# RWKV-7 and a routed expert layer on one core: the triangular inverse by 32x32 blocks in place of 128x128 block diagonal operands

## The chip, the core and the metric

The kernel runs on one core of a Trainium2 chip. The metric is the device time of one execution in microseconds; lower is better. All data are fp32 where the rows say f32. In the rows PE is TensorE's matmul, PEld its weight load, DVE VectorE, ACT ScalarE, POOL GpSimd, SP SyncE.

## What is computed

Two layers follow each other. The first is the RWKV-7 recurrence over 768 steps, for 4 batch elements and 8 heads of 40 features; its output, 3072 rows of 320 features, goes through a router that sends each row to one of 8 experts.

```python
for t in range(S):                      # 768 steps, per batch element and head
    y[t]  = r[t] @ state.T
    Sa    = state @ a[t]
    state = state * w[t] - outer(Sa, b[t]) + outer(v[t], k[t])
x = y as (3072, 320)
logits = normalised(x) @ normalised(expert_emb).T / tau
e = argmax(logits); gate = softmax(logits)[e]
out = gate * (relu(x @ w1[e]) @ w2[e])
```

## The kernel before, in words

The recurrence is taken in chunks of L = 32 steps. With the decays of a chunk multiplied into a, k and b, a chunk needs the inverse of a unit lower triangular 32x32 matrix I + tril(a b'), per head, and after it only small matrix products with the state. A tile holds four chunks of one batch element side by side on the 128 partitions; there are 24 tiles. The matrix between the steps of a tile is therefore block diagonal: four blocks of 32x32 in 128x128, for each of 8 heads.

`prepare` (line 192) does all of a tile that needs no state: the decays (lines 199 to 231), the turned inputs `ln`, `an`, `kn`, `bn` (237), the masked products `ne`, `ge`, `fe` (248, 251), then the inverse (286 to 306), then `te`, `gv` and `pt` (306 to 324). `advance` (326) carries the state through the tile's four chunks: per chunk `u_ps` (349), `un` (353), `s_ps` (357 and 362), the new state (367, 368), the turned state `sn` (374, 376) and `y_ps` (378); after the chunks come `ut`, `he` and the last part of `y_ps` (387 to 391), the router's logits and the store of `x_rows` (397 on). While a tile is in `advance`, the next is in `prepare`: both are generators, called in turn, and a scheduler lays the instructions of both out on each engine's queue, which the engine then runs in that order.

The inverse is grown by doubling the block size, in four levels after a first step (loop at line 294). The current inverse, transposed, stands compactly in `xt`, 128 partitions by 8 heads by 32 columns. One level is:

- VectorE turns `xt` in 32x32 blocks into `xn` (281), and GpSimd spreads `xn` into the block diagonal `xe`, 128x128 per head, with zeros off the diagonal (270, called at 295).
- TensorE takes 8 products, one per head, of the block diagonal `ne` with `xt` into `w_ps` (298); ScalarE copies them to `ws` (300).
- TensorE takes 8 products of `xe` with `ws` into `x_ps` (303); VectorE puts the level's entries into `xt` (304).

So a tile has 8 such groups of products, four of `w_ps` and four of `x_ps`. In the trace each fp32 product is two matmuls with a weight load each: 8 products are 16 matmuls. These are called passes here. Rows give the block of the array that a pass uses as rows times columns: 128\*128 for `w_ps`, 40\*32 for `u_ps`.

The expert stage (line 573 on) comes after all tiles: 31 blocks of 128 rows, each gathered, multiplied by its expert's two matrices, and scattered.

Of the kernel before, what the change touches and what calls it, by code (L numbers as in the profile page):

```python
# [14 lines left out]
AX = mybir.AxisListType  # L15
PSUM = bass.MemoryType.PSUM
CMAGIC = 12582912.0
# keeps a square root's argument in range; its root is lost in the 1e-6 that is added
TINY = 1e-30
P = 128  # L20
L = 32
NCK = P // L


def bc(ap, shape, axis):
    return ap.unsqueeze(axis).to_broadcast(shape)
# [3 lines left out]
def kernel(  # L30
# [12 lines left out]
    moe_w2: bass.AP,  # L43
    out: bass.AP,
):
    """RWKV-7 state recurrence in chunks of L steps, then top-1 routed experts.

    With lam_t the product of a chunk's decays before step t, per channel e,
        at = a lam_t,  kt = k / lam_(t+1),  bt = b / lam_(t+1)
        U  = (I + tril(at bt'))^-1 (at S' + tril(at kt') V)  # L50
        y  = lam (r S + tril(r V') kt - tril(r U') bt)
        S <- (S + V' kt - U' bt) lam_L
    where S is the state at the chunk's start and tril is strict.  A tile holds four chunks of
    one batch element on 128 partitions, so that matrices between steps are block diagonal.
    The kernel carries -U.  The inverse grows from blocks of one step to blocks of L steps:
    the off-diagonal block of a pair of inverted blocks X is that of X N X.
    """
    nc = tc.nc
    B, NT, D, H, _ = rT.shape
    S = NT * P  # L60
    N = B * S
# [33 lines left out]
    with ExitStack() as attn:  # L95
        cst = attn.enter_context(tc.tile_pool(name="cst", bufs=1))
        one = attn.enter_context(tc.tile_pool(name="one", bufs=1))
        two = attn.enter_context(tc.tile_pool(name="two", bufs=2))
# [3 lines left out]
        def bank(name):  # L102
            return mmp.tile([P, 512], FP32, tag="mm", name=name)

# [1 line left out]
        blk = cst.tile([P, P], FP32, name="blk")  # L106
        nc.vector.memset(blk, 0.0)
        for c in range(NCK):
# [28 lines left out]
        for j in range(L.bit_length() - 1):  # L137
            m = cst.tile([P, L], I32, name=f"level{j}")
# [7 lines left out]
        first = cst.tile([D, W1C], FP32, name="first")  # L146
# [2 lines left out]
        decay = cst.tile([D, W1C], FP32, name="decay")  # L149
        nc.vector.memset(decay[:, 0 :: L + 1], 0.0)  # L150

# [1 line left out]
        emb = two.tile([P, XW], FP32, tag="xr", name="emb")[0:E, 0:DM]  # L153
        nc.sync.dma_start(out=emb, in_=moe_expert_emb)
        tau = cst.tile([E, 1], FP32, name="tau")
# [15 lines left out]
        def h3(t):  # L171
            return t[:, 0:DM].rearrange("p (h d) -> p h d", h=H)

        def half(t):
            return t.rearrange("p (h x) -> p h x", h=4)

        state = {}
# [12 lines left out]
            loaded[g] = d  # L190

        def prepare(g, d):
            """Everything of a tile that needs no state, in parts."""
            d.update(loaded.pop(g))
            ck = "p (x t) -> p x t"

            # products of decays: before a step, and after it to the chunk's end
            body = decay[:, 0 : W1C - 1].rearrange(ck, t=L + 1)
            nc.scalar.copy(body[:, :, 1:], d["w"].rearrange("p h (c t) -> p (h c) t", t=L))
            lam = one.tile([D, W1C], FP32, tag="lam", name="lam")  # L200
            suf = one.tile([D, W1C], FP32, tag="suf", name="suf")
            nc.vector.tensor_tensor_scan(
                lam, decay, first, initial=0.0, op0=ALU.mult, op1=ALU.add
# [26 lines left out]
            nc.gpsimd.tensor_tensor(d["k"], d["k"], d["w"], ALU.mult)  # L230
            nc.gpsimd.tensor_tensor(d["b"], d["b"], d["w"], ALU.mult)

            # steps on partitions
            for nm, src in (("ln", lx), ("an", d["a"]), ("kn", d["k"]), ("bn", d["b"])):
                ps = h3(bank(f"{nm}_ps"))
                for h in range(H):
# [5 lines left out]
            def between(nm, lhs, rhs, mask, pool):  # L242
                t = pool.tile([P, H, P], FP32, tag=nm, name=nm)
                for q in range(2):
                    ps = half(bank(f"{nm}_ps"))
                    for j in range(4):
                        h = 4 * q + j
                        nc.tensor.matmul(  # L248
                            ps[:, j], lhsT=lhs[:, h], rhs=rhs[:, h], start=True, stop=True
                        )  # L250
                    nc.vector.tensor_tensor(
                        t[:, 4 * q : 4 * q + 4], ps, bc(mask, [P, 4, P], 1), ALU.mult
                    )
                return t

            d["between"] = between
            ne = between("ne", d["a"], d["b"], nlower, one)
# [7 lines left out]
            def c3(t):  # L265
                return t[:, 0 : H * L].rearrange("p (h j) -> p h j", h=H)

            def block_diagonal(x, nm):
                t = one.tile([P, H, P], FP32, tag=nm, name=nm)
                nc.gpsimd.tensor_tensor(  # L270
                    t.rearrange("p h (c j) -> p h c j", c=NCK),
                    bc(x, [P, H, NCK, L], 2),
                    bc(blk.rearrange("p (c j) -> p c j", c=NCK), [P, H, NCK, L], 1),
                    ALU.mult,
                )
                return t

            # inverse of I - N, transposed
            def turned(x):
                t = two.tile([P, H, L], FP32, tag="xn", name="xn")  # L280
                nc.vector.transpose(  # L281
                    t.rearrange("p h j -> p (h j)"), x.rearrange("p h j -> p (h j)")
                )
                return t

            xt = two.tile([P, H, L], FP32, tag="xt", name="xt")
# [5 lines left out]
            nc.vector.copy_predicated(xt, bc(levels[0], [P, H, L], 1), turned(nn))  # L292
            yield
            for m in levels[1:]:
                xe = block_diagonal(turned(xt), "xe")
                ps = c3(bank("w_ps"))
                for h in range(H):
                    nc.tensor.matmul(ps[:, h], lhsT=ne[:, h], rhs=xt[:, h], start=True, stop=True)  # L298
                ws = two.tile([P, H, L], FP32, tag="ws", name="ws")
                nc.scalar.copy(ws, ps)  # L300
                ps = c3(bank("x_ps"))
                for h in range(H):
                    nc.tensor.matmul(ps[:, h], lhsT=xe[:, h], rhs=ws[:, h], start=True, stop=True)  # L303
                nc.vector.copy_predicated(xt, bc(m, [P, H, L], 1), ps)  # L304
                yield
            te = block_diagonal(xt, "te")
# [10 lines left out]
            for q in range(2):  # L317
                ps = half(bank("pt_ps"))
                for j in range(4):
                    h = 4 * q + j  # L320
# [3 lines left out]
                nc.scalar.copy(pt[:, 4 * q : 4 * q + 4], ps[0:D])  # L324

        def advance(g, d):
            """Four chunks through the state; the tile's rows of x, their gates and experts."""
            b, i = groups[g]
            u_ps = h3(acc.tile([P, 512], FP32, tag="u", name="u_ps"))
            y_ps = h3(acc.tile([P, 512], FP32, tag="y", name="y_ps"))  # L330
            for h in range(H):
                nc.tensor.matmul(
                    u_ps[:, h], lhsT=d["te"][:, h], rhs=d["gv"][:, h],
                    start=(h == 0), stop=False, skip_group_check=True,
                )
            for h in range(H):
                nc.tensor.matmul(
                    y_ps[:, h], lhsT=d["fe"][:, h], rhs=d["kn"][:, h],
                    start=(h == 0), stop=False, skip_group_check=True,
# [3 lines left out]
            for c in range(NCK):  # L343
                r0 = L * c
                rows = slice(r0, r0 + L)
                last = i == NT - 1 and c == NCK - 1
                st = state[b]
                for h in range(H):
                    nc.tensor.matmul(  # L349
                        u_ps[rows, h], lhsT=d["pt"][:, h, rows], rhs=st[:, h],  # L350
                        start=False, stop=True, skip_group_check=True,
                    )
                nc.vector.tensor_scalar(un[rows], u_ps[rows], -1.0, None, ALU.mult)
                if not last:
                    s_ps = h3(acc.tile([P, 512], FP32, tag="s", name="s_ps"))[0:D]
                    for h in range(H):
                        nc.tensor.matmul(  # L357
                            s_ps[:, h], lhsT=d["kn"][rows, h], rhs=d["vn"][rows, h],
                            start=(h == 0), stop=False, skip_group_check=True,
                        )  # L360
                    for h in range(H):
                        nc.tensor.matmul(  # L362
                            s_ps[:, h], lhsT=d["bn"][rows, h], rhs=un[rows, h],
                            start=False, stop=True, skip_group_check=True,
# [12 lines left out]
                for h in range(H):  # L377
                    nc.tensor.matmul(  # L378
                        y_ps[rows, h], lhsT=d["r"][:, h, rows], rhs=sn[:, h],
                        start=False, stop=False, skip_group_check=True,  # L380
# [3 lines left out]
            for q in range(2):  # L384
                ps = half(bank("ut_ps"))
# [4 lines left out]
            for h in range(H):  # L390
                nc.tensor.matmul(
                    y_ps[:, h], lhsT=he[:, h], rhs=d["bn"][:, h],
                    start=False, stop=True, skip_group_check=True,
                )
            xr = two.tile([P, XW], FP32, tag="xr", name="xr")
            x = xr[:, 0:DM]
            nc.vector.tensor_tensor(h3(xr), y_ps, d["ln"], ALU.mult)

            # logits times the row's norm, the first of the largest, the gate
            xt_ps = bank("xt_ps")  # L400
            for j, (k0, kn) in enumerate(KC):
                nc.tensor.transpose(xt_ps[0:kn, j * P : j * P + P], xr[:, k0 : k0 + kn], ident)
# [4 lines left out]
            for j, (_, kn) in enumerate(KC):  # L407
                nc.tensor.matmul(
                    lg_ps, lhsT=xs[0:kn, j], rhs=embT[0:kn, j],
                    start=(j == 0), stop=(j == len(KC) - 1),  # L410
# [34 lines left out]
        for _ in prepare(0, ready):  # L445
            pass
        for g in range(NG):
            now, ready = ready, {}
            ahead = prepare(g + 1, ready) if g + 1 < NG else iter(())
            for _ in advance(g, now):  # L450
                next(ahead, None)
                next(ahead, None)
            for _ in ahead:
                pass
            if g % 2 == 1 and g // 2 < E:
                load_w2(g // 2)
# [7 lines left out]
        )  # L464
        nc.scalar.dma_start(out=w1_sb[0 : KC[2][1], e, 2], in_=moe_w1[e, 2 * P : DM])

# [1 line left out]
    with ExitStack() as rt:  # L468
        rp = rt.enter_context(tc.tile_pool(name="rp", bufs=1))
        rps = rt.enter_context(tc.tile_pool(name="rps", bufs=1, space=PSUM))  # L470
# [15 lines left out]
        for e in range(1, E):  # L486
# [3 lines left out]
        before = rp.tile([P, P], FP32, name="before")  # L490
# [7 lines left out]
            rk, lhsT=ones, rhs=cumx.rearrange("p s e -> p (s e)"),  # L498
            start=True, stop=False, skip_group_check=True,
# [3 lines left out]
            start=False, stop=True, skip_group_check=True,  # L503
# [16 lines left out]
        off = rp.tile([P, E], FP32, name="off")  # L520
# [11 lines left out]
        nc.vector.scalar_tensor_tensor(  # L532
            out=lo, in0=bk, scalar=-float(P), in1=dest, op0=ALU.mult, op1=ALU.add
        )
        # tokens as two parts under 64, which bfloat16 holds exactly, as it does 0 and 1
        shp = [P, NSLOT, NBLK]
        bm = rp.tile(shp, FP32, name="bm")
        nc.vector.tensor_tensor(bm, bc(io_p[:, 0:NBLK], shp, 1), bc(bk, shp, 2), ALU.is_equal)
# [11 lines left out]
        for s in range(NSLOT):  # L550
            nc.tensor.matmul(
                inv, lhsT=oh[:, s], rhs=rr[:, s].rearrange("p t k -> p (t k)"),
                start=(s == 0), stop=(s == NSLOT - 1),
# [16 lines left out]
        nc.vector.tensor_reduce(n1.unsqueeze(2), cm, axis=AX.X, op=ALU.add)  # L570
        nc.vector.tensor_scalar(eblk, n1, -1.0, None, ALU.add)

# [1 line left out]
    fw = ctx.enter_context(tc.tile_pool(name="fw", bufs=2))  # L574
    xins = [fw.tile([P, XW], FP32, name=f"xin{j}", bufs=1) for j in range(XBUF)]
    for t in xins:
# [140 lines left out]
```

## Time and profile before

| what | value |
|---|---|
| runs | 2609.22 and 8315.88 us, median 5462.55 |
| span of the profiled execution | 2610.3 us |
| TensorE busy in the span | 2519.8 us, 97% |
| mean granted TensorE clock | 0.589 of full speed |
| recurrence, up to the last store of `x_rows` | 0 to about 2212 us |
| expert stage | about 2213 to 2610 us |

The span, from the first instruction to the last, lies 1 us from the shorter of the two runs, so nothing of weight lies around it. The median of two runs is their mean and says nothing of either. A granted clock of 1.00 is 2.4 GHz, one of 0.50 is 1.2 GHz. The time that a row gives for matmuls goes to the modelled end of the last; where passes follow each other without a break, the distance from one start to the next is (time of n passes less the mean of one) / (n - 1).

### The profile page before, as it was taken

What the parts mean: (1) busy time and instruction counts of PE and PEld (TensorE: products, weight loads), DVE (VectorE), ACT (ScalarE), POOL (GpSimd) and SP (SyncE); (2) the same over time, 40 slices, a digit from 0 to 9 for tenths busy, and PEclk for the clock granted to TensorE, in tenths of its full rate; (3) what the DMA queues carried; (4) which work ended last, traced back from release to release, by engine and by line L of the source; (5) the groups of instructions that cost most, each with busy time, mean ns of one, the idle gap of its engine ahead of it and who ended that gap; (6) DMA issues with size and microseconds to landing.
All of it is one profiled execution on the core that took longest, in us unless ns stands there. A gap on an engine that the chain in (4) does not pass through costs nothing. (4 is left out here: it accounts for less than half of the span.)

```text
span 2610.3 us, 35907 instructions
## 1 busy us (share of the span) xinstructions
PE 2519.8 (97%) x15728; PEld 2211.9 (85%) x15728; DVE 692.9 (27%) x1374; ACT 375.9 (14%) x769; POOL 542.8 (21%) x336
## 2 busy tenths in 40 slices
PE   6999999999999999999999999999999998699998
PEld 5999999999999999999999999999999997255554
DVE  4232232233223223312322331332233122211111
ACT  1011111011111101111110111111011102011111
POOL 3122212212211221221122122212211210211111
PEclk9655555555555555555555555555555555799999
DMA  6000000000000000000000000000000001400000
GB/s 199 11 21 9 16 19 13 14 16 21 9 16 19 12 15 16 21 9 16 19 13 14 16 21 9 16 19 13 13 19 19 6 4 33 155 26 28 23 21 6
DMA packets 28411, 62.65 MB, mean 24 GB/s; under 512 B 4052, under 2 KB 18398, under 8 KB 28256
## 3 DMA queue, kind: packets, MB, share of 16 engines
q1 hardware_dynamic: 16320, 39.88, 5.0%
q10 hardware_dynamic: 8960, 12.58, 1.6%
q0 software_dynamic: 2976, 7.89, 1.0%
q8 instruction: 126, 2.06, 0.3%
q14 instruction: 29, 0.24, 0.0%
HBM read 53.60 MB, written 9.02 MB: 24 GB/s over the span
## 5 line engine op out<-in xcount | busy, mean ns | idle before, releaser
L270 POOL TENSOR_TENSOR xe<-xn,blk 128x1024 f32<-128x1024 f32 x96 | 226.9, 2364 | 1194.9 <-DVE xn L281 1011.3
L298 PE MATMUL w_ps<-xt,ne 128*128 128x32 f32 x1536 | 352.4, 403 | 3.2 <-DVE xt L304 3.2
L303 PE MATMUL x_ps<-ws,xe 128*128 128x32 f32 x1536 | 346.9, 402 | 8.1 <-ACT ws L300 7.3
L303 PEld LDWEIGHTS x_ps<-ws,xe 128*128 128x128 f32 x1536 | 334.7, 330 | 16.8 <-issue 7.4
L298 PEld LDWEIGHTS w_ps<-xt,ne 128*128 128x128 f32 x1536 | 336.4, 329 | 13.8 <-DVE xt L304 4.0
L618 PE MATMUL h_ps<-w_sb,xT 128*128 x372 | 184.6, 622 | 8.0 <-DMA w_sb<-in_moe_w_dram 8.0
L618 PEld LDWEIGHTS h_ps<-w_sb,xT 128*128 128x128 f32 x372 | 63.1, 189 | 113.7 <-issue 109.1
L304 DVE COPY_PREDICATED xt<-level,x_ps 128x256 f32<-128x256 int32 x96 | 42.4, 442 | 418.3 <-PE x_ps L303 418.3
L357 PE MATMUL s_ps<-vn,kn 32*40 32x40 f32 x1472 | 142.6, 265 | 0.0
L367 DVE TENSOR_TENSOR st<-s_ps,st 40x320 f32<-40x320 f32 x92 | 44.4, 483 | 367.0 <-PE s_ps L362 367.0
L300 ACT COPY ws<-w_ps 128x256 f32<-128x256 f32 x96 | 35.7, 372 | 728.4 <-PE w_ps L298 728.4
L645 PE MATMUL y_ps<-w_sb,hT 128*128 x496 | 138.8, 433 | 0.0
L376 ACT COPY sn<-sn_ps 40x320 f32<-40x320 f32 x96 | 40.2, 419 | 613.7 <-PE sn_ps L374 613.7
L357 PEld LDWEIGHTS s_ps<-vn,kn 32*40 32x40 f32 x1472 | 112.3, 171 | 19.0 <-issue 5.4
L349 PE MATMUL u_ps<-st,pt 40*32 40x40 f32 x1536 | 125.9, 264 | 0.0
L378 PE MATMUL y_ps<-sn,in_r 40*32 40x40 f32 x1536 | 122.6, 265 | 0.0
L378 PEld LDWEIGHTS y_ps<-sn,in_r 40*32 40x32 f32 x1536 | 106.6, 163 | 17.7 <-issue 13.2
L645 PEld LDWEIGHTS y_ps<-w_sb,hT 128*128 128x128 f32 x496 | 91.7, 190 | 34.2
L349 PEld LDWEIGHTS u_ps<-st,pt 40*32 40x32 f32 x1536 | 106.9, 162 | 16.2 <-issue 9.4
L362 PE MATMUL s_ps<-un,bn 32*40 32x40 f32 x1472 | 116.9, 263 | 0.4 <-DVE gs L434 0.4
L362 PEld LDWEIGHTS s_ps<-un,bn 32*40 32x40 f32 x1472 | 105.9, 176 | 7.1 <-issue 4.5
L248 PE MATMUL fe_ps<-in_r,in_v 40*128 40x128 f32 x384 | 105.7, 444 | 0.0
(180 smaller groups left out, 3301.4 us busy)
## 6 DMA issues: line engine op xcount, KB each, us to landing
w_sb<-in_moe_w_dram ACTq DMA_DIRECT2D x8, 1280.0 KB
w_sb<-in_moe_w_dram SPq DMA_DIRECT2D x8, 1024.0 KB
x_rows<-xr SPq DMA_DIRECT2D x24, 160.5 KB
in_w<-in_wT_dram SPq DMA_DIRECT2D x24, 160.0 KB
in_a<-in_aT_dram SPq DMA_DIRECT2D x24, 160.0 KB
in_k<-in_kT_dram SPq DMA_DIRECT2D x24, 160.0 KB
in_b<-in_bT_dram SPq DMA_DIRECT2D x24, 160.0 KB
in_v<-in_vT_dram SPq DMA_DIRECT2D x24, 160.0 KB
```

What stands on the lines that cost most here:

```text
L248: nc.tensor.matmul(ps[:, j], lhsT=lhs[:, h], rhs=rhs[:, h], start=True, stop=True)
L270: nc.gpsimd.tensor_tensor(t.rearrange("p h (c j) -> p h c j", c=NCK), bc(x, [P, H, NCK, L], 2), bc(blk.rearrange("p (c j) -> p c j", c=NCK ...
L298: nc.tensor.matmul(ps[:, h], lhsT=ne[:, h], rhs=xt[:, h], start=True, stop=True)
L303: nc.tensor.matmul(ps[:, h], lhsT=xe[:, h], rhs=ws[:, h], start=True, stop=True)
L304: nc.vector.copy_predicated(xt, bc(m, [P, H, L], 1), ps)
L349: nc.tensor.matmul(u_ps[rows, h], lhsT=d["pt"][:, h, rows], rhs=st[:, h], start=False, stop=True, skip_group_check=True,)
L357: nc.tensor.matmul(s_ps[:, h], lhsT=d["kn"][rows, h], rhs=d["vn"][rows, h], start=(h == 0), stop=False, skip_group_check=True,)
L362: nc.tensor.matmul(s_ps[:, h], lhsT=d["bn"][rows, h], rhs=un[rows, h], start=False, stop=True, skip_group_check=True,)
L367: nc.vector.tensor_tensor(new, s_ps, st, ALU.add)
L378: nc.tensor.matmul(y_ps[rows, h], lhsT=d["r"][:, h, rows], rhs=sn[:, h], start=False, stop=False, skip_group_check=True,)
L618: nc.tensor.matmul(ps, lhsT=d["xT"][0:kn, c], rhs=w1f[0:kn, ds(ek * (len(KC) * F) + c * F + q * 512, 512)], start=(c == 0), stop=(c == len ...
L645: nc.tensor.matmul(ps, lhsT=d["hT"][:, c], rhs=w2f[:, ds(d["ek"] * (FC * DM) + c * DM, DM)], start=(c == 0), stop=(c == FC - 1),)
```

## The change

`ne` is no longer used whole. Each head's product becomes four, one per diagonal block: weights, moving operand and result are those of one block, 32x32, on its 32 partitions. The second operand of the second product is `xd`, the turned `xt` itself, so the block diagonal `xe` is not built in the loop any more; `te` is still built that way once a tile. Lines after the loop move by 10.

```diff
             for m in levels[1:]:
-                xe = block_diagonal(turned(xt), "xe")
+                xd = turned(xt)
                 ps = c3(bank("w_ps"))
                 for h in range(H):
-                    nc.tensor.matmul(ps[:, h], lhsT=ne[:, h], rhs=xt[:, h], start=True, stop=True)
+                    for c in range(NCK):
+                        rows = slice(L * c, L * c + L)
+                        nc.tensor.matmul(
+                            ps[rows, h], lhsT=ne[rows, h, rows], rhs=xt[rows, h],
+                            start=True, stop=True, skip_group_check=True,
+                        )
                 ws = two.tile([P, H, L], FP32, tag="ws", name="ws")
                 nc.scalar.copy(ws, ps)
                 ps = c3(bank("x_ps"))
                 for h in range(H):
-                    nc.tensor.matmul(ps[:, h], lhsT=xe[:, h], rhs=ws[:, h], start=True, stop=True)
+                    for c in range(NCK):
+                        rows = slice(L * c, L * c + L)
+                        nc.tensor.matmul(
+                            ps[rows, h], lhsT=xd[rows, h], rhs=ws[rows, h],
+                            start=True, stop=True, skip_group_check=True,
+                        )
                 nc.vector.copy_predicated(xt, bc(m, [P, H, L], 1), ps)
                 yield
```

The scheduler lays the queues out anew. On TensorE's queue, in a tile in the middle of the program, the first two levels stood like this before; `x8` counts products, and `st_...` is the state of one batch element after one chunk:

```order
L374 MATMUL sn_ps<-ident,st_10036 40x40 x8
L298 MATMUL w_ps<-xt,ne 128x32 x8
L362 MATMUL s_ps<-un,bn 40x40 x8
L378 MATMUL y_ps<-sn,in_r 32x40 x8
L303 MATMUL x_ps<-ws,xe 128x32 x8
L357 MATMUL s_ps<-vn,kn 40x40
L349 MATMUL u_ps<-st_10118,pt 32x40 x8
L357 MATMUL s_ps<-vn,kn 40x40 x5
L298 MATMUL w_ps<-xt,ne 128x32 x8
L357 MATMUL s_ps<-vn,kn 40x40 x2
L362 MATMUL s_ps<-un,bn 40x40 x8
L303 MATMUL x_ps<-ws,xe 128x32 x8
```

The same two levels of a tile on TensorE's queue of the changed kernel:

```order
L384 MATMUL sn_ps<-ident,st_13532 40x40 x8
L300 MATMUL w_ps<-xt,ne 32x32
L388 MATMUL y_ps<-sn,in_r 32x40 x8
L300 MATMUL w_ps<-xt,ne 32x32 x8
L372 MATMUL s_ps<-un,bn 40x40 x8
L300 MATMUL w_ps<-xt,ne 32x32 x23
L310 MATMUL x_ps<-ws,xn 32x32 x32
L359 MATMUL u_ps<-st_13614,pt 32x40 x8
L367 MATMUL s_ps<-vn,kn 40x40 x6
L300 MATMUL w_ps<-xt,ne 32x32 x32
L367 MATMUL s_ps<-vn,kn 40x40 x2
L372 MATMUL s_ps<-un,bn 40x40 x4
```

The 8 products of a group are 32 now. In the first level the products of the state that stood between `w_ps` and `x_ps` have moved into `w_ps`, and `x_ps` follows `w_ps` at once.

The last level on TensorE's queue, before:

```order
L303 MATMUL x_ps<-ws,xe 128x32 x8
L357 MATMUL s_ps<-vn,kn 40x40 x6
L298 MATMUL w_ps<-xt,ne 128x32 x8
L357 MATMUL s_ps<-vn,kn 40x40 x2
L303 MATMUL x_ps<-ws,xe 128x32 x8
```

And the last level in the changed kernel:

```order
L310 MATMUL x_ps<-ws,xn 32x32 x32
L367 MATMUL s_ps<-vn,kn 40x40 x4
L372 MATMUL s_ps<-un,bn 40x40 x4
L300 MATMUL w_ps<-xt,ne 32x32 x32
L372 MATMUL s_ps<-un,bn 40x40 x4
L310 MATMUL x_ps<-ws,xn 32x32 x32
```

Four products stand between `w_ps` and `x_ps` where two stood. On GpSimd's queue a tile was

```order
L270 TENSOR_TENSOR xe<-xn,blk 128x1024 x4
L215 TENSOR_TENSOR in_w<-suf,inv_l 40x1024
L230 TENSOR_TENSOR in_k<-in_k,in_w 40x1024
L270 TENSOR_TENSOR te<-xt,blk 128x1024
L231 TENSOR_TENSOR in_b<-in_b,in_w 40x1024
L287 COPY xt<-icomp 128x256
```

and is, in the changed kernel, without the four `xe` and with `te` ahead of `in_w`:

```order
L270 TENSOR_TENSOR te<-xt,blk 128x1024
L215 TENSOR_TENSOR in_w<-suf,inv_l 40x1024
L287 COPY xt<-icomp 128x256
L230 TENSOR_TENSOR in_k<-in_k,in_w 40x1024
L231 TENSOR_TENSOR in_b<-in_b,in_w 40x1024
```

The four `xe` are gone, and `te` no longer stands behind `in_w` and `in_k`.

## Rows read from the trace of the kernel before

**Rows 1.** The page: busy time by engine, then granted clock in 40 slices.

```profile
PE 2519.8 (97%) x15728; PEld 2211.9 (85%) x15728; DVE 692.9 (27%) x1374; ACT 375.9 (14%) x769; POOL 542.8 (21%) x336
...
PEclk9655555555555555555555555555555555799999
```

**Rows 2.** Stretches: us; busy PE, PEld, DVE, ACT, POOL; granted clock; DMA; GB/s.

```profile
1085.40:1177.30 91.90, 91.12 (x610) 85.17 (x609) 25.43 (x48) 13.34 (x28) 19.66 (x10) 0.50 0.06 15
1177.30:1268.90 91.60, 90.82 (x611) 85.03 (x610) 25.43 (x48) 13.34 (x28) 19.66 (x10) 0.50 0.05 15
2250.00:2537.00 287.00, 287.00 (x975) 152.25 (x974) 49.30 (x125) 43.74 (x76) 48.50 (x48) 1.00 0.07 23
```

**Rows 3.** Waits: who waited for whom, us, times, longest.

```profile
POOL xe L270 <- DVE xn L281: 1011.3, 75, 25.4
ACT ws L300 <- PE w_ps L298: 728.4, 96, 15.8
...
PE x_ps L303 <- ACT ws L300: 7.3, 25, 0.6
```

**Rows 4.** Groups by line: busy us, mean ns of one, idle before.

```profile
L298 PE MATMUL w_ps<-xt,ne 128*128 128x32 f32 x1536 | 352.4, 403 | 3.2 <-DVE xt L304 3.2
L303 PE MATMUL x_ps<-ws,xe 128*128 128x32 f32 x1536 | 346.9, 402 | 8.1 <-ACT ws L300 7.3 <-POOL xe L270 0.8
...
L270 POOL TENSOR_TENSOR xe<-xn,blk 128x1024 f32<-128x1024 f32 x96 | 226.9, 2364 | 1194.9 <-DVE xn L281 1011.3 <-DVE lam_l L210 183.6
...
L349 PE MATMUL u_ps<-st,pt 40*32 40x40 f32 x1536 | 125.9, 264 | 0.0
```

**Rows 5.** TensorE in order of time, a tile's first level: start, us, passes.

```profile
1105.82 1.27 PE L349 MATMUL u_ps<-st,pt 40*32 40x40 f32 x16
1107.02 0.35 PE L357 MATMUL s_ps<-vn,kn 32*40 32x40 f32 x2
1107.30 0.72 PE L374 MATMUL sn_ps<-ident,st 40*40 40x40 f32 x8
1107.95 3.62 PE L298 MATMUL w_ps<-xt,ne 128*128 128x32 f32 x16
1111.50 1.29 PE L362 MATMUL s_ps<-un,bn 32*40 32x40 f32 x16
```

**Rows 6.** The same view, later in that tile: 8 columns against 128-wide weights.

```profile
1172.17 1.00 PE L408 MATMUL lg_ps<-embT,xs 128*128 128x8 f32 x4
```

**Rows 7.** Groups by line in 1172.1 to 1174.3: mean ns of one.

```profile
L408 PE MATMUL lg_ps<-embT,xs 128*128 128x8 f32 x4 | 1.0, 361 | 0.0
```

**Rows 8.** TensorE in order of time, first tile, alone: group after group.

```profile
41.58 3.60 PE L298 MATMUL w_ps<-xt,ne 128*128 128x32 f32 x16
45.73 3.59 PE L303 MATMUL x_ps<-ws,xe 128*128 128x32 f32 x16 [0.55 <-ACT ws L300]
```

**Rows 9.** A stretch of 2 us at the higher clock.

```profile
173.50:175.50 2.00, 2.00 (x36) 1.95 (x35) 1.50 (x1) 1.99 (x7) 0.00 (x0) 1.00 0.00 0
```

**Rows 10.** TensorE in that stretch, in order of time.

```profile
175.32 0.47 PE L349 MATMUL u_ps<-st,pt 40*32 40x40 f32 x8
```

**Rows 11.** Groups by line in 175.3 to 175.75: mean ns of one.

```profile
L349 PE MATMUL u_ps<-st,pt 40*32 40x40 f32 x8 | 0.5, 201 | 0.0
```

**Rows 12.** TensorE in order of time: where the second and the last tile's `prepare` begin.

```profile
83.00 0.69 PE L237 MATMUL ln_ps<-ident,lx 40*128 40x40 f32 x8
...
2088.45 0.69 PE L237 MATMUL ln_ps<-ident,lx 40*128 40x40 f32 x8
```

## The prediction, made before the changed kernel ran

> **What bounds the kernel now.** I read the page first: TensorE is busy for 97% of the span, no other engine for more than 27%, and from the third slice to the end of the recurrence the granted clock stands near half [rows 1]. Then the stretches: two tiles in the middle have TensorE busy 91.12 of 91.90 us at a granted clock of 0.50, 1.2 GHz, while the experts run at 1.00, 2.4 GHz [rows 2]. So the recurrence is a queue of TensorE work without gaps, (2088.45 - 83.00) / 22 = 91.2 us a tile [rows 12]. The waits agree: the longest are those of GpSimd and ScalarE for work ahead of them, and TensorE waited for ScalarE's `ws` 7.3 us in all [rows 3]. The change touches one stage only, the inverse; the experts' 400 us stay.
>
> What does a pass cost there? For `w_ps`, 16 passes take 3.62 us with 0.402 for one, so the next starts (3.62 - 0.40) / 15 = 0.214 us after the last [rows 4, 5]. These passes move 32 columns. `lg_ps` moves 8 against weights as wide, and its passes follow at (1.00 - 0.361) / 3 = 0.213 [rows 6, 7]. So the moving columns are not what costs: the load of 128 weight columns is, 1.67 ns a column. `u_ps`, with 32 weight columns and 40 moving ones, goes at (1.27 - 0.264) / 15 = 0.067, which is 1.67 ns for each of 40 [rows 4, 5]. A pass thus takes 1.67 ns for each column of the larger of the two, and the other is hidden. A group of `w_ps` or `x_ps` is 16 x 0.214 = 3.42 us, and 8 of them are 27.4 of a tile's 91.2 us.
>
> **The change, part by part.**
>
> The products. A group has 32 products, 64 passes, of 32 weight columns and 32 moving ones. One after the other these take 32 x 1.67 = 0.0533 us each, and 64 of them 3.41 us: exactly what the group costs now. A quarter of the width and four times the number cancel. All that can be won is that passes on different blocks, which share neither rows nor columns of the array, run side by side. No row of before has two such passes in succession, so I bound it. Above: 0.0533 us a pass, no overlap, nothing won. Below: four abreast, 0.0533 / 4 = 0.0133, a group of 0.85 us. Four abreast is unlikely from the order itself: the two passes of a product stand next to each other on the same block and cannot overlap, so that only the second pass of one block and the first of the next can, which halves the cost at best, to 0.027, as long as starts are in order. The quickest succession of fp32 passes with their loads in any row is that of `u_ps` in a short stretch at the higher clock: (0.47 - 0.201) / 7 = 0.038 us [rows 9 to 11]. Loads and matmuls can be fed at least that fast. I take 0.038: between the ends, and what a row has shown. A group is then 64 x 0.038 = 2.43 us, 0.99 less, and 8 groups give 7.9 us a tile.
>
> The page "TensorE: Matmul & The Clock Gate" of the Trainium skill (Part 3: Packing small matmuls) says that matmuls on different 32x32 blocks start some 4 ns apart, and gives 10.6 times the rate for 16 blocks with 512 moving columns. It says nothing of two-pass fp32 products with 32 columns, and no run here shows it. The same section says that a weight load overlaps with a matmul under way only where their rows differ. The trace speaks against that: `w_ps` loads and multiplies on the same 128 rows, and in turn they would take 0.213 + 0.053 = 0.267 us, where 0.214 is measured [rows 5].
>
> Changes of block shape. Between passes of different shape the array stands still for a moment: 16 passes of `u_ps` from 1105.82 would end their turn at 1106.89, and `s_ps` starts at 1107.02; `w_ps` from 1107.95 at 1111.37, and `s_ps` starts at 1111.50 [rows 5]. That is 0.13 us each. In the new order a tile has 43 of them where it had 42, so 0.1 us a tile is added.
>
> Waits. In the first level the changed order puts `x_ps` straight behind `w_ps`. The first tile shows what that costs: `x_ps` starts 45.73 - 41.58 = 4.15 us after `w_ps`, and 4.15 - 15 x 0.214 = 0.94 us after its last pass [rows 8]. Of these 0.05 are the last pass itself, so 0.9 us are lost per tile, with all of the state's products queued behind on TensorE and nothing else waiting that is late. In the last level four products, 8 passes, stand between: 8 x 0.067 + 2 x 0.13 = 0.80 of the 0.94, so 0.15 is lost. At the other levels the products between cover it. Together with the shapes that is 1.2 us a tile.
>
> GpSimd. 96 `xe` of 2.36 us go, 227 us of GpSimd's time [rows 4]. TensorE waited for them 0.8 us in the whole run, so their cover is TensorE's own queue and I count nothing. `te` moves ahead, which nobody waits for. VectorE's and ScalarE's instructions of a level stay as they are, and so do the DMAs.
>
> Sum: (7.9 - 1.2) x 24 tiles = 161 us off the span of 2610.3, so 2449; I say **2450 us**. The span lies 1 us from the shorter of the two runs. The median, 5462.55, is the mean of that run and one of 8315.88, so the forecast stands to the 2609.22 alone.
>
> The clock. TensorE was busy for 99% of a tile and was granted half the clock [rows 2]; it stays as busy in my sum, so I leave the clock there.
>
> **Rivals.**
>
> *Nothing overlaps.* The loads could go one at a time whatever block they are for; each pass then takes 0.0533 us and a group 3.41. For it: loads alone set the pace of `w_ps`. Against: these loads were all for the same rows. The time is 2610 + 24 x 1.2 = 2639 us, no change. A second way to the same end is a least time per matmul that small ones cannot go under. At the higher clock it is at most 0.038 us [rows 10, 11], and at the lower one nothing here bounds it below 0.067. Anything over 0.047 leaves the gain under 2%; at 0.050 a group is 3.2 us and the time 2610 - 24 x (1.76 - 1.2) = 2597.
>
> The page "TensorEngine Tiling (Array Packing)" of the Trainium skill (Instruction Overhead) has that rule: each matmul has about 60 cycles of overhead, and the factor should not be taken from a dimension that is small already. At 1.2 GHz an estimate by it is 0.050 us, the 2597 above.
>
> *More than two abreast.* If second passes do not hold up the next block's first, down to 0.0133 us: (8 x 2.57 - 1.2) x 24 = 465 us, 2145. Against it stand the order of the passes and a group so short that covers thin out. I take 2145 to 2310 for this case, where 2310 is half the serial cost: (8 x 1.71 - 1.2) x 24 = 300.
>
> *Slower: a change of block stops the array* as a change of shape does. There are 32 in a group, 256 in a tile. At the full 0.13 us that is 33.3 us more a tile, with the 1.2 above 24 x 34.5 = 828, so 3438 us. For it: every change of rows or columns that rows 5 show costs 0.13. Against: there the shape changes too, and `s_ps` or `u_ps` change nothing else. It decides early: with no overlap, 2% is 52 us, 2.2 a tile, 1.0 beyond the waits, or 0.004 us a change.
>
> **How the numbers follow.** My forecast's case, 0.026 to 0.047 us a pass, is 2310 to 2560 us: chance 0.45. More abreast: 0.12. No overlap or a least time, 2560 to 2660: 0.27. Slower by a cost of each change of block: 0.16. The range is 2230 to 2690: it leaves out half of the second case and two thirds of the last, under 0.2. A measurement of this kernel tells about 2% from no change, 52 us: faster 0.45 + 0.12 = 0.57, within 0.27, slower 0.16.
>
> **What would show it.** In the profile after, a group's 64 passes: at 2.43 us I am right, at 3.4 nothing overlaps, at 7 or more each change of block costs. A tile should be 84.5 us. TensorE should wait for `ws` about 24 x 0.9 us where it waited 7.3, GpSimd should be busy about 316 us, and the experts' 400 us the same. I am wrong if the granted clock in the tiles leaves 0.50, if the passes' pace in the trace does not carry the sum, or if another engine than TensorE ends a tile.

## The result, and the profile after

The changed kernel takes 2148.9 us, the median of two runs of 2144.23 and 2153.58. Against the kernel before it is 0.823 of the time, 95% interval 0.815 to 0.831; timed once more, with four runs of its own and seven of the kernel before, 0.8216, interval 0.8203 to 0.8230. The run of 8315.88 us of the kernel before is left out of these ratios. The prediction said 2450 us and 2230 to 2690: faster was right, the size was not. The time is that of the rival with more than two blocks abreast, 2145 us, to which it gave a chance of 0.12.

The page after, first the busy time by engine, then the granted clock in 40 slices, as in [rows 1]:

```profile
PE 2034.7 (95%) x24944; PEld 1725.1 (81%) x24944; DVE 692.4 (32%) x1374; ACT 377.9 (18%) x769; POOL 298.1 (14%) x240
...
PEclk9655555555555555555555555555555558999999
```

TensorE has 9216 passes more and is busy 485 us less. VectorE and ScalarE work as long as they did. GpSimd loses 245 us: 227 of `xe`, and 18 because the 24 `te` that remain take 2.35 us each where they took 3.09. Two tiles in the middle and a stretch of experts, as in [rows 2] (us; busy PE, PEld, DVE, ACT, POOL; granted clock; DMA; GB/s):

```profile
998.40:1071.30 72.90, 71.51 (x995) 65.53 (x994) 25.40 (x48) 13.61 (x29) 9.36 (x6) 0.50 0.07 20
1071.30:1143.60 72.30, 70.91 (x994) 65.04 (x993) 25.41 (x48) 13.03 (x28) 9.36 (x6) 0.50 0.08 20
1783.40:2070.00 286.60, 286.60 (x976) 152.73 (x976) 50.07 (x126) 43.73 (x76) 48.97 (x48) 1.00 0.08 23
```

TensorE still sets the pace of a tile, with 98% of it busy, at the same half clock; the experts are what they were. Where the second and the last tile's `prepare` begin, as in [rows 12] (start, us, passes):

```profile
69.58 0.69 PE L237 MATMUL ln_ps<-ident,lx 40*128 40x40 f32 x8
...
1638.70 0.69 PE L237 MATMUL ln_ps<-ident,lx 40*128 40x40 f32 x8
```

A tile is (1638.70 - 69.58) / 22 = 71.3 us, 19.8 less than the 2005.45 / 22 = 91.16 of before, where 84.5 was predicted. 24 x 19.8 is 476 us, and the span is 468 us shorter. So the whole of the gain lies in the tiles. This is TensorE in order of time over the first two levels of a tile, as in [rows 5]:

```profile
1020.71 0.31 PE L300 MATMUL w_ps<-xt,ne 32*32 32x32 f32 x2
1021.34 1.27 PE L388 MATMUL y_ps<-sn,in_r 40*32 40x40 f32 x16 [0.33 <-ACT sn L386]
1022.54 0.43 PE L300 MATMUL w_ps<-xt,ne 32*32 32x32 f32 x16
1022.91 1.28 PE L372 MATMUL s_ps<-un,bn 32*40 32x40 f32 x16
1024.12 0.86 PE L300 MATMUL w_ps<-xt,ne 32*32 32x32 f32 x46
1025.46 1.08 PE L310 MATMUL x_ps<-ws,xn 32*32 32x32 f32 x64 [0.48 <-ACT ws L305]
1026.47 1.27 PE L359 MATMUL u_ps<-st,pt 40*32 40x40 f32 x16
1027.67 1.02 PE L367 MATMUL s_ps<-vn,kn 32*40 32x40 f32 x12
1028.61 1.08 PE L300 MATMUL w_ps<-xt,ne 32*32 32x32 f32 x64
```

A group is 1.08 us where it was 3.62. And the groups by line, as in [rows 4] (busy us, mean ns of one, idle before):

```profile
L300 PE MATMUL w_ps<-xt,ne 32*32 32x32 f32 x6144 | 121.1, 238 | 3.9 <-DVE xt L314 3.9
L310 PE MATMUL x_ps<-ws,xn 32*32 32x32 f32 x6144 | 104.0, 237 | 16.5 <-ACT ws L305 12.9 <-issue 3.7
```

With 0.238 us for one pass, the next starts (1.08 - 0.238) / 63 = 0.0134 us after the last. That is a quarter of the 0.0533 that a pass takes alone. The four blocks run fully abreast: 64 x 0.0133 = 0.85 us a group, 2.57 less than before. 8 groups give 20.6 us a tile, of which 19.8 are seen; waits and changes of block shape take the rest.

### The profile page after: what moved, and what is told of

The parts are those of the page before. It is cut to its first block, busy times and chain, and to the rows that moved or that the text cites. A ratio compares the mean times of both kernels' runs of the same rounds, so it can differ in the third digit from the quotient of the medians.

```text
span 2142.5 us, 54098 instructions
## 1 busy us (share of the span) xinstructions
PE 2034.7 (95%) x24944; PEld 1725.1 (81%) x24944; DVE 692.4 (32%) x1374; ACT 377.9 (18%) x769; POOL 298.1 (14%) x240
## 5 line engine op out<-in xcount | busy, mean ns | idle before, releaser
L270 POOL TENSOR_TENSOR te<-xt,blk 128x1024 f32<-128x1024 f32 x24 | 56.4, 2349 | 976.1 <-DVE xt L314 976.1
L367 PE MATMUL s_ps<-vn,kn 32*40 32x40 f32 x1472 | 130.1, 265 | 0.0
L372 PE MATMUL s_ps<-un,bn 32*40 32x40 f32 x1472 | 126.1, 263 | 0.4 <-DVE gs L444 0.4
L300 PE MATMUL w_ps<-xt,ne 32*32 32x32 f32 x6144 | 121.1, 238 | 3.9 <-DVE xt L314 3.9
L310 PE MATMUL x_ps<-ws,xn 32*32 32x32 f32 x6144 | 104.0, 237 | 16.5 <-ACT ws L305 12.9
L300 PEld LDWEIGHTS w_ps<-xt,ne 32*32 32x32 f32 x6144 | 99.7, 149 | 18.6 <-DVE xt L314 4.3
L310 PEld LDWEIGHTS x_ps<-ws,xn 32*32 32x32 f32 x6144 | 90.9, 150 | 25.7 <-ACT ws L305 16.3
L251 DVE TENSOR_TENSOR he<-he_ps,upper 128x512 f32<-128x512 f32 x48 | 32.8, 684 | 230.1 <-PE he_ps L248 230.1
L248 PE MATMUL fe_ps<-in_r,in_v 40*128 40x128 f32 x384 | 98.4, 435 | 0.0
L322 PE MATMUL gv_ps<-vn,ge 128*128 128x40 f32 x384 | 92.3, 416 | 0.0
```

The source lines that it names most:

```text
L248: nc.tensor.matmul(ps[:, j], lhsT=lhs[:, h], rhs=rhs[:, h], start=True, stop=True)
L270: nc.gpsimd.tensor_tensor(t.rearrange("p h (c j) -> p h c j", c=NCK), bc(x, [P, H, NCK, L], 2), bc(blk.rearrange("p (c j) -> p c j", c=NCK ...
L300: nc.tensor.matmul(ps[rows, h], lhsT=ne[rows, h, rows], rhs=xt[rows, h], start=True, stop=True, skip_group_check=True,)
L310: nc.tensor.matmul(ps[rows, h], lhsT=xd[rows, h], rhs=ws[rows, h], start=True, stop=True, skip_group_check=True,)
L322: nc.tensor.matmul(gv_ps[:, h], lhsT=ge[:, h], rhs=d["vn"][:, h], start=True, stop=True)
L367: nc.tensor.matmul(s_ps[:, h], lhsT=d["kn"][rows, h], rhs=d["vn"][rows, h], start=(h == 0), stop=False, skip_group_check=True,)
```

## The experiments

The prediction had held four abreast unlikely because of the order of the passes. Two theories were set against each other. Theory 1: passes start in the order of the queue, and only neighbours overlap. Theory 2: TensorE looks ahead over its queue and starts a pass whose block is free, past others that wait. Each run below is the changed kernel with the edit shown. The four runs that change the order, and the one with the rows of one block, were executed once each: their times have no interval, and the readings rest on the time of a group in the trace.

**All heads of a block in succession.** Both loops over products are exchanged:

```diff
-                for h in range(H):
-                    for c in range(NCK):
+                for c in range(NCK):
+                    for h in range(H):
```

> The changed kernel with the two inner loops exchanged: the 8 heads of one block follow each other, then the next block. The changed kernel ran 2144 us with 64 passes of a group in 1.08 us. Theory 1, passes start in the order of the queue and only neighbours on different blocks overlap: 16 passes in succession share a block, each 0.053 us, a group is 3.4 us again, and the time is 2144 + 192 groups x 2.5 = about 2620 us. Theory 2, TensorE looks ahead over the queue and takes any pass whose block is free: with sight over more than 16 passes two blocks run abreast, a group is 1.7 us, the time about 2310; with sight over a whole group nothing changes, 2144.

It took 2534.65 us. One group in this run, TensorE in order of time (start, us, passes):

```profile
986.84 3.06 PE L310 MATMUL x_ps<-ws,xn 32*32 32x32 f32 x64 [0.46 <-ACT ws L305]
```

(3.06 - 0.238) / 0.0533 = 53 pass times from first to last start, where 63 is one after the other: neither theory's number. Eleven passes in the middle of that group's first 16, which are all on the first block:

```profile
986.97 0.77 PE L310 MATMUL x_ps<-ws,xn 32*32 32x32 f32 x11
```

(0.77 - 0.238) / 10 = 0.0532 us from one to the next. So passes on one block do run one after the other, and the gain does come from blocks side by side. But 10 of the 63 steps are gone, 3.4 at each of the 3 changes of block, where bare order saves at most one at each. So there is a look ahead, and it is short.

**Two heads of a block in succession.**

```diff
-                for h in range(H):
-                    for c in range(NCK):
+                for h0 in range(0, H, 2):
+                    for c, h in [(c, h0 + j) for c in range(NCK) for j in range(2)]:
```

> The changed kernel with two heads of one block in succession, then the next block, so four passes of a block stand together. Theory 1 (order of the queue, neighbours only): at best the last pass of a block runs beside the first of the next, a pass costs 0.027 us or more, a group 1.7 us or more, the time 2310 us or more. Theory 2 (a look ahead): over 12 passes or more the four blocks still run abreast, 2144 us.

It took 2145.09 us. A group in this run, in the same view:

```profile
1026.79 1.15 PE L310 MATMUL x_ps<-ws,xn 32*32 32x32 f32 x64 [0.47 <-ACT ws L305]
```

Four passes of a block stand together here. With starts in order each of the 15 changes of block saves one of 63 steps, so a group could not be under 48 x 0.0533 = 2.6 us, more than the 1.7 of the expectation. It is 0.91 from first to last start, and the time is that of the changed kernel. Theory 1 falls.

**Two blocks in turn.**

```diff
-                for h in range(H):
-                    for c in range(NCK):
+                for c0 in range(0, NCK, 2):
+                    for h, c in [(h, c0 + j) for h in range(H) for j in range(2)]:
```

> The changed kernel with blocks 0 and 1 in turn for all heads, then blocks 2 and 3. Theory 1: two blocks abreast, 0.027 us a pass, a group 1.7 us, the time 2144 + 192 x 0.86 = 2309 us. Theory 2 with a sight of some 30 passes: between that and 2144, with starts in threes or fours at the seam.

It took 2261.34 us. A group in this run, in the same view:

```profile
1013.31 1.74 PE L310 MATMUL x_ps<-ws,xn 32*32 32x32 f32 x64 [0.47 <-ACT ws L305]
```

1.50 us from first to last start: two abreast, 31 steps of 0.0533, less 3 at the one change from blocks 0 and 1 to 2 and 3. The same short sight shows at the seam.

**Four heads of a block in succession**, to test the size of the look ahead with a number given first. The edit is as in the run with two, with steps of four.

> The changed kernel with four heads of one block in succession, 8 passes, then the next block. With all 8 heads in succession a group measured 2.82 us from first to last start, 53 times 0.0533, where 63 would be no overlap: about 3.4 passes overlapped at each of the 3 changes of block. If TensorE starts a pass past at most 3 or 4 that wait, 7 changes of block overlap 7 x 3.4 = 24 passes: 40 x 0.0533 = 2.1 us a group, and 2144 + 192 x 1.29 = about 2390 us. If it sees much further, as the unchanged time with runs of two could also mean: 2144 to 2200 us.

It took 2367.32 us. A group in this run, in the same view:

```profile
907.09 2.31 PE L310 MATMUL x_ps<-ws,xn 32*32 32x32 f32 x64 [0.46 <-ACT ws L305]
```

2.07 us from first to last start against 2.1, and the time is 1% under the one that the short look ahead gave. So the next block's passes start while some 3 or 4 of the block before still wait, and that is enough for the order of the changed kernel: a product's second pass waits for its block, and the next three blocks' first passes go past it.

The 3 or 4 are passes of one block, not all that wait. These are the passes that start in the first 0.05 us of the group shown above for two heads in succession:

```profile
1026.79 0.30 PE L310 MATMUL x_ps<-ws,xn 32*32 32x32 f32 x4 [0.47 <-ACT ws L305]
```

A block takes 0.0533 us for a pass, so these four are on four blocks. With four passes of each block in succession on the queue, the last of them has gone past nine that wait, three of each block. What in TensorE sets the limit is not shown.

**Four products from the rows of one block.** The four passes of a head differ in their columns alone:

```diff
-                            ps[rows, h], lhsT=ne[rows, h, rows], rhs=xt[rows, h],
+                            ps[rows, h], lhsT=ne[0:L, h, rows], rhs=xt[0:L, h],
...
-                            ps[rows, h], lhsT=xd[rows, h], rhs=ws[rows, h],
+                            ps[rows, h], lhsT=xd[0:L, h], rhs=ws[0:L, h],
```

> The changed kernel with both operands of all four products of a head taken from the rows of block 0, so that the four passes differ in their columns alone; the result of the inverse is then block 0's for all blocks. If different rows are needed for passes to run side by side: 0.053 us a pass, a group 3.4 us, about 2620 us. If different columns are enough: 2144 us.

It took 2146.01 us. A group in this run, in the same view:

```profile
955.88 1.08 PE L310 MATMUL x_ps<-ws,xn 32*32 32x32 f32 x64 [0.48 <-ACT ws L305]
```

Different columns are enough. Whether different rows with the same columns are enough was not tried.

**`xe` kept.** The products by blocks, but with the second operand taken from `xe`, so that GpSimd builds it as before:

```diff
-                xd = turned(xt)
+                xe = block_diagonal(turned(xt), "xe")
...
-                            ps[rows, h], lhsT=xd[rows, h], rhs=ws[rows, h],
+                            ps[rows, h], lhsT=xe[rows, h, rows], rhs=ws[rows, h],
```

> The changed kernel with GpSimd's xe built again in every level, and x_ps taking its 32x32 blocks from xe instead of the turned xt; products and their overlap are as in the changed kernel. If the four xe of a tile were worth nothing, as the prediction said of the kernel before: 2144 us. If their cover, w_ps of 3.4 us, is gone with w_ps at 0.85: in the second level some 2.2 us of TensorE work stand between the start of w_ps and x_ps, in the fourth 1.3, where turning and xe take some 3.1; 2.7 us a tile, 24 x 2.7 = 65, so about 2210 us, and TensorE's idle time ahead of x_ps put down to GpSimd.

It took 2214.04 us, 0.8487 of the kernel before, interval 0.8466 to 0.8509. From the waits in this run (us, times, longest):

```profile
POOL xe L270 <- DVE xn L281: 803.9, 89, 24.5
...
PE x_ps L310 <- POOL xe L270: 68.4, 50, 7.1
```

TensorE waits 68 us for `xe` where it waited 0.8 before the change, and the time is 67 us over the 2147.13 us of the changed kernel. That the two are so close is partly chance. By the pages TensorE is idle for 153.3 us where the changed kernel has 107.8, only 45 more, because its waits for `ws` and `sn` there, 12.9 and 6.8 us, do not come up here; and it is busy 2055.1 us, 20 more, on a queue that was laid out anew, for which no run shows the reason. `xe` was worth nothing only as long as `w_ps` covered it.

**`w_ps` alone by blocks.** `x_ps` and `xe` stay as before the change.

```diff
-                            ps[rows, h], lhsT=xd[rows, h], rhs=ws[rows, h],
-                            start=True, stop=True, skip_group_check=True,
+                    nc.tensor.matmul(ps[:, h], lhsT=xe[:, h], rhs=ws[:, h], start=True, stop=True)
```

> Only w_ps by blocks; x_ps and xe as before the change. If the gain is the passes' pace alone, half of it comes: 2144 + 24 x 4 x 2.57 = 2390 us; with the waits for xe of the run before, 2390 to 2460 us.

It took 2418.49 us, 0.9263 of before, interval 0.9243 to 0.9283. The two groups by line in this run (busy us, mean ns of one, idle before):

```profile
L308 PE MATMUL x_ps<-ws,xe 128*128 128x32 f32 x1536 | 347.7, 402 | 68.4 <-POOL xe L270 68.4
...
L300 PE MATMUL w_ps<-xt,ne 32*32 32x32 f32 x6144 | 110.2, 238 | 3.2 <-DVE xt L309 3.2
```

The half that was left costs what it cost, the other half has the new pace, and the waits for `xe` are there as in the run before. Half of the products thus give 192 of the change's 467 us, not 234. By the pages TensorE is busy 2264.9 us, 255 less than before, but idle 151.6, 61 more: it waits for `xe`, which `x_ps` still needs and `w_ps` no longer covers.

**Four more groups by blocks.** `gv`, and `te`, `fe` and `he` as weights:

```diff
             for h in range(H):
-                nc.tensor.matmul(
-                    u_ps[:, h], lhsT=d["te"][:, h], rhs=d["gv"][:, h],
-                    start=(h == 0), stop=False, skip_group_check=True,
-                )
+                for c in range(NCK):
+                    rows = slice(L * c, L * c + L)
+                    nc.tensor.matmul(
+                        u_ps[rows, h], lhsT=d["te"][rows, h, rows], rhs=d["gv"][rows, h],
+                        start=(h == 0), stop=False, skip_group_check=True,
+                    )
...
```

> The changed kernel with four more groups by blocks: gv, and te, fe and he as weights into u_ps and y_ps, whose 128x128 operands hold zeros off the diagonal too. Each is 16 passes of 0.214, 3.42 us, and becomes 64 passes of 40 moving columns, 64 x 0.0667 / 4 = 1.07 us. A tile loses 4 x 2.35 = 9.4 us: 2144 - 24 x 9.4 = 1918 us if TensorE's queue still sets the pace; 1950 to 2000 if waits for other engines take part of it; 2144 if passes that add into a bank under way do not overlap.

It took 1923.44 us, 0.7371 of before, interval 0.7355 to 0.7386. The group of `fe`, which adds into a bank that others add to later, in order of time in this run:

```profile
862.43 1.29 PE L356 MATMUL y_ps<-kn,fe 32*32 32x40 f32 x64
```

(1.29 - 0.262) / 63 = 0.0163 us a pass, a quarter of the 0.067 of 40 columns. Half of the group of `he`, which adds to the same bank after others have, goes at (0.76 - 0.261) / 31 = 0.0161:

```profile
857.93 0.76 PE L412 MATMUL y_ps<-bn,he 32*32 32x40 f32 x32
```

**The masked products by blocks as well.** `ne`, `ge`, `fe` and `he` are computed for the diagonal blocks alone, and kept compactly:

```diff
             def between(nm, lhs, rhs, mask, pool):
-                t = pool.tile([P, H, P], FP32, tag=nm, name=nm)
+                t = pool.tile([P, H, L], FP32, tag=nm, name=nm)
...
+                            ps[rows, h], lhsT=lhs[:, h, rows], rhs=rhs[:, h, rows],
...
-                    u_ps[rows, h], lhsT=d["te"][rows, h, rows], rhs=d["gv"][rows, h],
+                    u_ps[rows, h], lhsT=d["xt"][rows, h], rhs=d["gv"][rows, h],
```

> As the run before (e7), and the masked products ne, ge, fe and he computed by blocks too, 40 rows and 32 columns, stored compactly, one mask instruction of 256 columns instead of two of 512, without the reduction to nn, and with xt itself as the weights in place of te in u_ps. These four groups share their rows and differ in columns alone. If different columns are enough, as the run with the rows of one block (e6) says, each of them goes from 3.42 to 64 x 0.0133 = 0.85 us: 10.2 us a tile less than e7's kernel, 24 x 10.2 = 246, about 1670 us if TensorE still sets the pace, up to 1780 with waits. If they do not overlap, e7's time.

It took 1666.59 us, 0.6381 of before, interval 0.6369 to 0.6393, against 1670 expected: this beats both kernels. Timed beside it, the changed kernel again:

> The changed kernel itself once more, timed beside the run before: 2144 us if the first two executions hold, 17 to 19% under the kernel before.

It took 2147.13 us. Here is TensorE of the kernel with all blocks, in order of time, where the group of `ne` ends and that of `ge` begins:

```profile
831.19 0.72 PE L254 MATMUL ne_ps<-in_b,in_a 40*32 40x32 f32 x62
831.74 0.20 PE L254 MATMUL ge_ps<-in_a,in_k 40*32 40x32 f32 x1
831.74 0.19 PE L254 MATMUL ne_ps<-in_b,in_a 40*32 40x32 f32 x1
831.75 0.20 PE L254 MATMUL ge_ps<-in_a,in_k 40*32 40x32 f32 x1
831.75 0.19 PE L254 MATMUL ne_ps<-in_b,in_a 40*32 40x32 f32 x1
831.77 1.01 PE L254 MATMUL ge_ps<-in_a,in_k 40*32 40x32 f32 x61
```

On the queue all 64 passes of `ne` stand ahead of all of `ge`. Two of `ge` start before the last two of `ne`; in 22 of the run's 24 tiles some of `ge` start before the last of `ne`. This is the look ahead itself, seen between two groups whose names tell them apart. That an engine runs its queue in the order laid out, as the description of the kernel ahead of the prediction has it, does not hold for TensorE.

## Why the prediction was wrong, step by step

**What bounds the kernel: right.** A queue of TensorE work at half clock before and after. The pace of 1.67 ns for each column of the larger operand held too: a block alone runs at 0.0533 us a pass in the run with all heads in succession.

**The products: the step that failed.** It read: four abreast is unlikely from the order itself, since the two passes of a product stand next to each other on the same block, "as long as starts are in order". They are not. The runs with two and four heads in succession show starts past 3 or 4 waiting passes of a block, and the group of the changed kernel is 0.85 us, not 2.43. The term was 7.9 us a tile and is 20.6. The choice within the bounds failed with it: 0.038 us was the quickest succession in any row of before, but that row has all its passes on one block, where the block's own time sets the pace. It bounded what one block can do, and I used it for what the queue can feed. The bound below, 0.0133, is what came.

**A least time, and the order of starts.** By the Trainium skill's page "TensorEngine Tiling (Array Packing)", Instruction Overhead, each matmul has an overhead of about 60 cycles; by the prediction's estimate that would have left the time nearly unchanged, at 2597 us. Starts 0.0134 us apart show that no such least time stands between starts on different blocks. The Trainium skill's other page, "TensorE: Matmul & The Clock Gate" (Part 3: Packing small matmuls), was the better guide, since the four blocks do run side by side in fp32 with 32 columns; but it also says that matmuls start strictly in order, and the rows of `ne` and `ge` above show the opposite.

**Changes of shape: right.** After 16 passes of `u_ps` from 1026.47, due to end at 1027.54, `s_ps` starts at 1027.67: 0.13 us, as before. Their number was one short: by the trace a tile in the middle has 51 changes of the weights' block shape where it had 49, two more and not one, which is another 0.1 us. A change of block within a shape costs nothing, which ends the slower rival.

**Waits: right in place, too large.** `x_ps` does wait for `ws` in the first level. The last pass of `w_ps` starts at 1024.12 + 0.86 - 0.238 = 1024.74 and `x_ps` at 1025.46, 0.72 us later where 0.94 was taken. In the whole run TensorE waits 12.9 us for `ws`, where 24 x 0.9 was expected. In the fourth level no wait shows. One that I did not name came in: `y_ps` waits 0.33 us for `sn`, since a single product of `w_ps` now stands between the two.

**GpSimd: right for the kernel before, and no more.** I named TensorE's queue as the cover of `xe`, and did not price what it costs once the change itself has taken most of that cover away: 67 us, if `xe` had stayed.

**The clock: right.** 0.50 in the tiles before and after.

**The sum.** With 0.0133 in place of 0.038 it was worked out among the rivals, and gave 2145 us; 2144.23 and 2153.58 were measured. That the first lies within 1 us is partly luck: a tile loses 0.7 us to waits and changes of shape where 1.2 was taken, which is worth 12 us, and the span shows 468 us of the 476 that 24 such tiles would give. The reading of what bounds the kernel and the lower bound of a pass stood. The case that I chose did not: its mechanism, starts in order, was wrong, and with it the size of the products' term and the chances, 0.45 and 0.27 for cases that rested on starts in order or on loads one at a time, 0.12 for the one that came.

## What to carry to other kernels

Where a matrix on 128 partitions is block diagonal, its zeros are paid for in weight columns: four 32x32 products on different columns of the array take the time of one, and here eight more groups took it as well, down to 0.638 of the time. In these runs the order on the queue mattered only where more than about 3 waiting passes of one block stood ahead of the next block's: two heads of a block in succession cost nothing, four cost 220 us. And a price of zero for a helper on another engine holds for the cover that it has now: see first whether the change takes that cover away, and keep the helper's removal in the same change.

## What the hardware showed that was not expected

- TensorE starts matmuls out of queue order, past some 3 or 4 that wait for one block: 3.4 steps are saved per change of block with 16 passes of a block in a row, and a group with 8 in a row takes 2.07 us against 2.1 worked out from it. With 4 in a row all four blocks are at work within 0.05 us, past nine that wait.
- Four fp32 passes that share their 32 rows and differ in columns alone run abreast, at 0.0134 us a pass, as those do that differ in both.
- Passes that add into a bank under way overlap in the same way, at 0.0161 us for 40 columns.
